# A chunked recurrence and an expert layer: products over a head's 40 entries, issued by groups of heads or alternating between two halves of the array's rows

## The chip, the core and the metric

The kernel runs on one core of a Trainium2 chip. The metric is the device time of one execution in microseconds, the median over runs of the same kernel. Engines are named as the profile names them: PE is TensorE (PEld its weight loads), DVE VectorE, ACT ScalarE, POOL GpSimd, SP SyncE, which here only issues DMAs.

## What is computed

Everything is float32. A recurrence (4 batches, 8 heads, 768 steps, 40 entries a head) carries a 40 x 40 state a head; its outputs, laid side by side, are 3072 tokens of 320 entries, and a two-level gate sends each token to one of 16 experts.

```python
for t in range(S):
    y[:, :, t] = np.einsum('bhd,bhde->bhe', rt, state)
    Sa = np.einsum('bhde,bhe->bhd', state, at)
    state_decay = state * wt[:, :, None, :] - np.einsum('bhd,bhe->bhde', Sa, bt)
    state = state_decay + np.einsum('bhd,bhe->bhde', vt, kt)
...
h = np.maximum(xg[mask_e] @ w1[g, e], 0.0)
ye = h @ w2[g, e]
out[tok_idx] = combined[:, None] * ye
```

## The kernel before

**Part one** computes the recurrence in chunks of 128 steps: 6 chunks a batch, 24 in all, the four batches taking turns. A chunk holds all 8 heads. The inputs of a chunk lie with a head's 40 entries on the partitions: even heads on partitions 0 to 39, odd heads on 64 to 103, four heads of each kind side by side along the free axis. `blk(g)` (L174) gives the partitions of the even (g = 0) or the odd heads (g = 1). A matmul over the 40 entries therefore uses the lower half of the array's rows for an even head and the upper half for an odd one.

`product` (L222) makes, for one of the two groups, four 128 x 128 matrices, one a head, in one PSUM bank (a tile of the tag `big`, of which five are in turn), and VectorE then multiplies the bank by a triangular mask into SBUF (L228). It is called eight times a chunk: for GT (L233), E (L235) and MT (L251) at the chunk's front, and for NT (L324) at its end. A float32 matmul stands in the trace as two passes, so the four matmuls of one call are eight records of PE and eight of PEld.

The other steps of a chunk, in the order in which PE takes them:

- The gate's logits of the chunk before: transposes of its tokens (L120) and small matmuls (L131). The scheduler sets the first products of the new chunk between them.
- The products GT and E; then the right-hand side (L260, L263), which needs GT with its mask.
- E's rows are summed, bounded and scaled (L239 to L244, VectorE and GpSimd), then E is transposed on PE (L247) and copied by ScalarE (L249).
- The product MT; then transposes of b, k and the running products (L217).
- Seven levels of the inverse: in each PE squares E and its transpose (L273, L282), ScalarE or VectorE copies the squares to SBUF, and PE applies the transposed square to U (L293), which VectorE adds up (L299).
- U is transposed (L304, copied at L307); the next state's products (L314, L315) go to VectorE, which updates the state ST (L318, L341) with qo (L320); the product NT needs the transposed U; the new state is transposed (L346).
- The chunk's outputs are summed from three products (L328, L332 with MT, L334 with NT) and scaled by VectorE (L336).

The tile framework's scheduler sets the order on each engine from the program's order and the dependences; the input loads of later chunks run on SP's queue, with three sets of input tiles in turn.

**Part two** chooses the experts (mostly VectorE), scatters the tokens by expert to DRAM, and then takes 39 tiles of 128 rows through the two expert matrices (L558, L566). The loops at L389 and L429 run zero times for these inputs.

Of the kernel before, what the change touches and what calls it, by code (L numbers as in the profile page):

```python
# [9 lines left out]
F32 = mybir.dt.float32  # L10
I32 = mybir.dt.int32
AX = mybir.AxisListType
ALU = mybir.AluOpType
# [3 lines left out]

# The chunked form of the recurrence divides by running products of w and inverts I + T by
# powers of T. Both are accurate while w stays within these bounds (128 factors make 1e-15 to
# 1e15) and no row of |T| sums to more than T_MAX. If an input breaks them anywhere, the  # L20
# recurrence is computed again a step at a time, in the reference's order.
W_MIN, W_MAX, T_MAX = 0.765, 1.3, 1.0
# [3 lines left out]
def kernel(  # L26
# [15 lines left out]
    nc = tc.nc  # L42
    P = 128
    B, H, D, S = rT.shape
    DM = H * D
    C = P
    NC = S // C
    NN = B * NC
    NP = H // 2
    HW = 64  # L50
    G, Eg = w1.shape[0], w1.shape[1]
# [7 lines left out]
    NK = len(KO)  # L59
    XW = DM + 2  # L60
    NT = (NTOK + NE * (P - 1)) // P
# [10 lines left out]
    def big(shape):  # L72
        return psum.tile(shape, F32, tag="big", name="big", bufs=5)
# [3 lines left out]

# [1 line left out]
    ident = cpool.tile([P, P], F32, name="ident")  # L79
    make_identity(nc, ident)  # L80
    ones = cpool.tile([P, P], F32, name="ones")
    nc.gpsimd.memset(ones, 1.0)
    # up[s, t] = 1 for s < t; low[t, s] = 1 for s < t
    up = cpool.tile([P, P], F32, name="up")
    nc.gpsimd.affine_select(out=up, in_=ones, compare_op=ALU.is_ge, fill=0.0, base=-1,
                            pattern=[[1, P]], channel_multiplier=-1)
    low = cpool.tile([P, P], F32, name="low")
    nc.gpsimd.affine_select(out=low, in_=ones, compare_op=ALU.is_ge, fill=0.0, base=-1,
                            pattern=[[-1, P]], channel_multiplier=1)
    up4 = up[:, None, :].broadcast_to([P, NP, P])  # L90
    low4 = low[:, None, :].broadcast_to([P, NP, P])

# [1 line left out]
    # A row of x_all is a token: its vector, its gate weight and its number.  # L94
    x_all = cpool.tile([P, NN, XW], F32, name="x_all")
# [8 lines left out]

    # Rows sorted by expert, each expert's share filled up to whole tiles. Rows that no token
    # takes keep a zero vector and a number beyond the last token.
    xs = dpool.tile([NT * P, XW], F32, name="xs")
# [8 lines left out]
    def transpose_x(pool, src):  # L116
        """[128 tokens, DM] -> [128, NK, 128 tokens]."""
        pt = big([P, NK, P])
        for ko, (k0, kn) in enumerate(KO):
            nc.tensor.transpose(pt[:kn, ko, :], src[:, k0:k0 + kn], ident)  # L120
        t = pool.tile([P, NK, P], F32, tag="xT", name="xT", bufs=2)
        nc.vector.tensor_copy(out=t[:, :NK - 1, :], in_=pt[:, :NK - 1, :])  # L122
        kn = KO[-1][1]
        nc.scalar.copy(out=t[:kn, NK - 1, :], in_=pt[:kn, NK - 1, :])  # L124
        return t
# [8 lines left out]

# [1 line left out]
    # With P_t the product of w over the chunk's steps before t and Q_t that product through t,  # L136
    # A = a P, K = k / Q, B = b / Q and S the state at the chunk's start:
    #   (I + T) U = A S' + G V,         T[t, s] = B_s . A_t,  G[t, s] = K_s . A_t   (s < t)
    #   Y = P (R S + M K - N B),        M[t, s] = r_t . v_s,  N[t, s] = r_t . u_s   (s < t)
    #   next S = (S + V' K - U' B) Q_last  # L140
    # and (I + T)^-1 = (I - T)(I + T^2)(I + T^4)... exactly, T being strictly triangular.
    with ExitStack() as part:
# [14 lines left out]
        for i in range(2):  # L157
            t = pers.tile([P, H, HW], F32, name=f"U{i}")
            nc.gpsimd.memset(t[:, :, D:], 0.0)
            U_pad.append(t)  # L160
        # The states of a pair of heads stand as the two diagonal blocks of a square that is zero
        # elsewhere: ST with the second axis of a state on the partitions, SN with the first.
        ST, SN = [], []
# [10 lines left out]
        def blk(h):  # L174
            return slice((h % 2) * HW, (h % 2) * HW + D)

        for u in range(NN):
# [4 lines left out]
            if u < NB:  # L182
                # the partitions that no head's rows take
                for nm in "wakbvr":
                    for q0 in (32, 96):
                        nc.any.memset(d[nm][q0:q0 + 32], 1.0 if nm == "w" else 0.0)
                nc.any.memset(d["pq"][:, :, 0:1], 1.0)
# [9 lines left out]

            # the running products of w (within its bounds), and a, k, b scaled by them
            nc.vector.tensor_reduce(out=w_max[:, n:n + 1], in_=d["w"], axis=AX.XY, op=ALU.max)
# [21 lines left out]

            def product(lhs, rhs, g, mask, name, bufs):  # L222
                ps = big([P, NP, P])
                for q in range(NP):
                    nc.tensor.matmul(ps[:, q, :], lhsT=lhs[blk(g), q, :], rhs=rhs[blk(g), q, :],  # L225
                                     start=True, stop=True)
                t = sb.tile([P, NP, P], F32, name=name, bufs=bufs)
                nc.vector.tensor_tensor(t, ps, mask, op=ALU.mult)  # L228
                return t

            # group 0 has the even heads, group 1 the odd ones
            GR = range(2)
            GT = [product(Kt, At, g, up4, "GT", 4) for g in GR]  # L233
            # T and its transpose; a row beyond its bound is scaled down to it
            E = [product(At, Bt, g, low4, "E", 6) for g in GR]  # L235
            ET = []
            for g in GR:
# [12 lines left out]
                ET.append(t)  # L250
            MT = [product(Vt, Rt, g, up4, "MT", 4) for g in GR]  # L251
            nB = natural(Bt, "nB", -1.0)
            Kn = natural(Kt, "Kn", 1.0)
            Pn = natural(Pm, "Pn", 1.0)

            # the right-hand side, then a factor of the inverse at a time
            ps = small([P, H, D])
# [50 lines left out]

            # the next state
            if c < NC - 1:  # L310
# [11 lines left out]

            # what the chunk returns
            NTm = [product(UT, Rt, g, up4, "NT", 4) for g in GR]  # L324
            ps = small([P, H, D])
# [25 lines left out]

        # how often the bounds are broken
        bad = pers.tile([P, 4], F32, name="bad")
# [13 lines left out]

# [1 line left out]
    with ExitStack() as part:  # L369
# [4 lines left out]
        BH = B * H  # L374
        # partition (q, b, h) holds rows q DQ .. (q + 1) DQ of the state of (b, h)
        st = sq.tile([P, DQ, D], F32, name="st")
# [56 lines left out]

# [1 line left out]
    with ExitStack() as part:  # L435
# [12 lines left out]
        def choose(vals, name):  # L448
            """The first largest of each token's values as a one-hot, and its softmax weight."""
            sh = [P, NN, G]  # L450
# [32 lines left out]

        # each token's rank within its expert, then its row in xs
        ohf = oh.rearrange("p n e -> p (n e)")
# [31 lines left out]

        # each tile's expert
        past = gp.tile([P, NT, NE], F32, name="past")
# [11 lines left out]

# [1 line left out]
    with ExitStack() as part:  # L533
# [66 lines left out]
```

## Time and profile before

| | |
|---|---|
| median of the runs shown (2 runs: 2348.99 and 2349.27 us) | 2349.13 us |
| the profiled execution: span from the first to the last instruction | 2344.1 us |
| of that, PE's matmuls busy | 2137.4 us (91%) |
| VectorE, ScalarE, GpSimd busy | 636.2, 416.2, 188.8 us |
| mean granted clock of PE | 0.806 |

The span is the profiled execution's own time; what lies around it is the difference to the median, 5 us. A record of PE begins when its pass begins; its end is modelled, and consecutive passes overlap in the records, so the pace of a stage is read from the starts. The granted clock is a share of the full 2.4 GHz: 0.50 is 1.2 GHz.

### The profile page before, as it was taken

Reading aid. Unit: us, or ns where it says so; the run is one execution under the profiler, and the core shown is the slowest. Engines: PE = TensorE matmul, PEld = TensorE weight load, DVE = VectorE, ACT = ScalarE, POOL = GpSimd, SP = SyncE. Lnnn points to the kernel's source line nnn. Section 1 sums busy time; section 2 is a strip of 40 time slices with the busy share of each in tenths; the row PEclk is TensorE's granted clock in tenths of the full one; section 3 lists DMA queues with packets and bytes.
Section 4 is the critical chain, followed back from the end, with each engine's and each line's share of the span. In section 5 each row is a group of like instructions: output and inputs, shape, how many; then the busy total and the mean of one; then the engine's idle time right before and its main releaser. Section 6 shows DMA issues by size and latency. Waiting matters only on the chain. (4 is left out here: it accounts for less than half of the span.)

```text
span 2344.1 us, 32451 instructions
## 1 busy us (share of the span) xinstructions
PE 2137.4 (91%) x13731; PEld 1943.0 (83%) x13731; DVE 636.2 (27%) x1156; ACT 416.2 (18%) x766; POOL 188.8 (8%) x190
## 2 busy tenths in 40 slices
PE   4999999999999999999999999999505999999998
PEld 3999999999999999999999999999404677777676
DVE  6423333332333333233333232222300111111111
ACT  2222222121222212122212122222000000000000
POOL 3000000000000000000000000000021000000000
PEclk9878876687877868787767787777656999999999
DMA  6000000000000000000000000000042666666661
GB/s 186 21 12 18 21 17 19 20 18 12 18 18 18 21 21 18 12 18 18 18 21 18 12 13 18 4 1 1 29 155 88 212 212 215 200 202 217 205 212 51
DMA packets 143699, 152.68 MB, mean 65 GB/s; under 512 B 33529, under 2 KB 129534, under 8 KB 143552
## 3 DMA queue, kind: packets, MB, share of 16 engines
q1 hardware_dynamic: 133824, 136.21, 18.9%
q10 hardware_dynamic: 6704, 6.46, 1.0%
q0 software_dynamic: 3024, 7.90, 0.9%
q8 instruction: 111, 1.82, 0.3%
q14 instruction: 36, 0.29, 0.0%
HBM read 136.22 MB, written 16.78 MB: 65 GB/s over the span
## 5 line engine op out<-in xcount | busy, mean ns | idle before, releaser
L558 PE MATMUL big<-xT,w1s 128*128 128x128 f32 x1872 | 338.9, 312 | 25.3 <-DVE xT L122 24.6
L558 PEld LDWEIGHTS big<-xT,w1s 128*128 128x128 f32 x1872 | 259.3, 191 | 108.0 <-DVE xT L122 34.7
L293 PE MATMUL small<-U,ET 128*128 128x40 f32 x2688 | 345.9, 290 | 0.6 <-ACT ET L276 0.4
L293 PEld LDWEIGHTS small<-U,ET 128*128 128x128 f32 x2688 | 340.8, 205 | 2.3 <-ACT ET L276 0.5
L273 PE MATMUL big<-ET,E 128*128 128x128 f32 x2304 | 336.6, 292 | 0.0
L273 PEld LDWEIGHTS big<-ET,E 128*128 128x128 f32 x2304 | 300.7, 204 | 0.0
L282 PE MATMUL big<-E,ET 128*128 128x128 f32 x1920 | 266.0, 284 | 0.0
L276 ACT COPY ET<-big 128x512 f32<-128x512 f32 x288 | 168.8, 586 | 481.2 <-PE big L273 481.2
L282 PEld LDWEIGHTS big<-E,ET 128*128 128x128 f32 x1920 | 247.3, 201 | 0.0
L299 DVE TENSOR_TENSOR U<-U,small 128x320 f32<-128x320 f32 x168 | 80.7, 480 | 457.4 <-PE small L293 457.4
L566 PE MATMUL small<-w2s,hT 128*128 128x320 f32 x624 | 180.5, 443 | 0.0
L566 PEld LDWEIGHTS small<-w2s,hT 128*128 128x128 f32 x624 | 116.6, 192 | 48.9 <-issue 1.6
L244 POOL TENSOR_TENSOR E<-E,fit 128x512 f32<-128x512 f32 x48 | 48.9, 1039 | 1199.5 <-DVE fit L242 1188.8
L561 DVE TENSOR_SCALAR hT<-big 128x512 f32<-128x512 f32 x39 | 27.0, 692 | 342.6 <-PE big L558 342.6
L124 ACT COPY xT<-big 64x128 f32<-64x128 f32 x63 | 16.3, 259 | 565.2 <-DVE xT L122 565.2
L120 PE MATMUL big<-ident,xt 128*128 128x128 f32 (+1 forms) x117 | 19.6, 277 | 96.4 <-DMA xt<-xs 96.4
L225 PE MATMUL big<-in_a,in_k 40*128 40x128 f32 x384 | 89.0, 447 | 18.1 <-DMA in_r<-in_rT_dram 18.1
L120 PEld LDWEIGHTS big<-ident,xt 128*128 128x128 f32 (+1 forms) x117 | 14.2, 133 | 105.4 <-DMA xt<-xs 97.5
L334 PE MATMUL small<-nB,NT 128*128 128x40 f32 x384 | 98.6, 351 | 0.0
L225 PEld LDWEIGHTS big<-in_a,in_k 40*128 40x128 f32 x384 | 75.1, 322 | 27.8 <-POOL in_k L212 18.1
L332 PE MATMUL small<-Kn,MT 128*128 128x40 f32 x384 | 94.4, 339 | 0.0
L263 PE MATMUL small<-vn,GT 128*128 128x40 f32 x384 | 94.1, 402 | 0.0
(166 smaller groups left out, 2302.5 us busy)
## 6 DMA issues: line engine op xcount, KB each, us to landing
w2s<-in_w_dram SPq DMA_DIRECT2D x39, 1280.0 KB
w1s<-in_w_dram SPq DMA_DIRECT2D x39, 1024.0 KB
w1s<-in_w_dram SPq DMA_DIRECT2D x39, 256.0 KB
xs<-blank ACTq DMA_DIRECT2D x1, 6279.0 KB
xt<-xs SPq DMA_DIRECT2D x39, 161.0 KB
vn<-in_v_dram SPq DMA_DIRECT2D x24, 160.0 KB
in_w<-in_wT_dram SPq DMA_DIRECT2D x48, 80.0 KB
in_a<-in_aT_dram SPq DMA_DIRECT2D x48, 80.0 KB
```

Of the source, the lines that this page charges most:

```text
L225: nc.tensor.matmul(ps[:, q, :], lhsT=lhs[blk(g), q, :], rhs=rhs[blk(g), q, :], start=True, stop=True)
L244: nc.gpsimd.tensor_tensor(E[g], E[g], fit.broadcast_to([P, NP, P]), op=ALU.mult)
L263: nc.tensor.matmul(ps[:, 2 * i + j, :], lhsT=GT[j][:, i, :], rhs=vn[:, 2 * i + j, :], start=(c == 0), stop=(c == 0 or j == 1))
L273: nc.tensor.matmul(ps[:, q, :], lhsT=E[g][:, q, :], rhs=ET[g][:, q, :], start=True, stop=True)
L276: nc.scalar.copy(out=t, in_=ps)
L282: nc.tensor.matmul(ps[:, q, :], lhsT=ET[g][:, q, :], rhs=E[g][:, q, :], start=True, stop=True)
L293: nc.tensor.matmul(ps[:, h, :], lhsT=ET[h % 2][:, h // 2, :], rhs=U[:, h, :], start=True, stop=True)
L299: nc.vector.tensor_tensor(nx, U, ps, op=ALU.add if lv else ALU.subtract)
L332: nc.tensor.matmul(o, lhsT=MT[j][:, i, :], rhs=Kn[:, i, blk(j)], start=(c == 0), stop=False)
L334: nc.tensor.matmul(o, lhsT=NTm[j][:, i, :], rhs=nB[:, i, blk(j)], start=False, stop=(c == 0 or j == 1))
L558: nc.tensor.matmul(ps[:, f, :], lhsT=w1s[:kn, ko, (f0 + f) * P:(f0 + f + 1) * P], rhs=xT[:kn, ko, :], start=(ko == 0), stop=(ko == NK - 1))
L566: nc.tensor.matmul(ps, lhsT=hT[:, f, :], rhs=w2s[:, f, :], start=(f == 0), stop=(f == FQ - 1))
```

## The change

`product` no longer takes the group. It takes two PSUM banks at once, one for the even and one for the odd heads, and issues the eight matmuls head by head: even, odd, even, odd. When all eight stand in the program, the two masks follow. It returns both results, so the four places that called it twice call it once. The number of matmuls, masks and banks is the same. (The change also blanks comment lines, so line numbers behind `product` rise by 6: L263 becomes L269, L334 becomes L340; the matmuls of `product` stand at L228, the masks at L233.)

```diff
-            def product(lhs, rhs, g, mask, name, bufs):
-                ps = big([P, NP, P])
+            def product(lhs, rhs, mask, name, bufs):
+                pss = [big([P, NP, P]) for _ in range(2)]
                 for q in range(NP):
-                    nc.tensor.matmul(ps[:, q, :], lhsT=lhs[blk(g), q, :], rhs=rhs[blk(g), q, :],
-                                     start=True, stop=True)
-                t = sb.tile([P, NP, P], F32, name=name, bufs=bufs)
-                nc.vector.tensor_tensor(t, ps, mask, op=ALU.mult)
-                return t
+                    for g in range(2):
+                        nc.tensor.matmul(pss[g][:, q, :], lhsT=lhs[blk(g), q, :],
+                                         rhs=rhs[blk(g), q, :], start=True, stop=True)
+                out = []
+                for g in range(2):
+                    t = sb.tile([P, NP, P], F32, name=name, bufs=bufs)
+                    nc.vector.tensor_tensor(t, pss[g], mask, op=ALU.mult)
+                    out.append(t)
+                return out
...
-            GT = [product(Kt, At, g, up4, "GT", 4) for g in GR]
+            GT = product(Kt, At, up4, "GT", 4)
...
-            E = [product(At, Bt, g, low4, "E", 6) for g in GR]
+            E = product(At, Bt, low4, "E", 6)
...
-            MT = [product(Vt, Rt, g, up4, "MT", 4) for g in GR]
+            MT = product(Vt, Rt, up4, "MT", 4)
...
-            NTm = [product(UT, Rt, g, up4, "NT", 4) for g in GR]
+            NTm = product(UT, Rt, up4, "NT", 4)
```

The order of PE at GT and E of one chunk in the middle of the program (the products of in_a with in_k are GT, of in_b with in_a E; the numbers behind `big_` tell the banks' tiles apart), before:

```order
L225 MATMUL big_4061<-in_a0_98,in_k0_99 128x128 x3
L131 MATMUL small_4031<-wg_77,xT_4028 128x20 x2
L225 MATMUL big_4061<-in_a0_98,in_k0_99 128x128
L131 MATMUL small_4031<-wg_77,xT_4028 128x20
L225 MATMUL big_4068<-in_a0_98,in_k0_99 128x128 x4
L225 MATMUL big_4075<-in_b0_100,in_a0_98 128x128 x4
L225 MATMUL big_4082<-in_b0_100,in_a0_98 128x128 x4
```

and with the change, the first twelve rows of the same place:

```order
L228 MATMUL big_4061<-in_a0_98,in_k0_99 128x128
L228 MATMUL big_4062<-in_a0_98,in_k0_99 128x128
L228 MATMUL big_4061<-in_a0_98,in_k0_99 128x128
L131 MATMUL small_4031<-wg_77,xT_4028 128x20 x2
L228 MATMUL big_4062<-in_a0_98,in_k0_99 128x128
L131 MATMUL small_4031<-wg_77,xT_4028 128x20
L228 MATMUL big_4061<-in_a0_98,in_k0_99 128x128
L228 MATMUL big_4062<-in_a0_98,in_k0_99 128x128
L228 MATMUL big_4061<-in_a0_98,in_k0_99 128x128
L228 MATMUL big_4062<-in_a0_98,in_k0_99 128x128
L228 MATMUL big_4075<-in_b0_100,in_a0_98 128x128
L228 MATMUL big_4076<-in_b0_100,in_a0_98 128x128
```

The logits stay behind the third matmul, which is now one of the lower half again, and the halves alternate throughout; E follows in the same way.

The order of VectorE at the same place, from the masks of GT to the scale of E's rows, before:

```order
L228 TENSOR_TENSOR GT_4066<-big_4061,up_70 128x512
L228 TENSOR_TENSOR GT_4073<-big_4068,up_70 128x512
L228 TENSOR_TENSOR E_4080<-big_4075,low_72 128x512
L239 TENSOR_REDUCE t_sum_88<-E_4080 128x4
L228 TENSOR_TENSOR E_4087<-big_4082,low_72 128x512
L242 TENSOR_SCALAR fit_4090<-t_sum_88 128x4
L239 TENSOR_REDUCE t_sum_88<-E_4087 128x4
L243 RECIPROCAL fit_4090<-fit_4090 128x4
L242 TENSOR_SCALAR fit_4102<-t_sum_88 128x4
L243 RECIPROCAL fit_4102<-fit_4102 128x4
```

and with the change:

```order
L233 TENSOR_TENSOR GT_4071<-big_4061,up_70 128x512
L233 TENSOR_TENSOR GT_4073<-big_4062,up_70 128x512
L233 TENSOR_TENSOR E_4085<-big_4075,low_72 128x512
L233 TENSOR_TENSOR E_4087<-big_4076,low_72 128x512
L245 TENSOR_REDUCE t_sum_88<-E_4085 128x4
L245 TENSOR_REDUCE t_sum_88<-E_4087 128x4
L248 TENSOR_SCALAR fit_4090<-t_sum_88 128x4
L248 TENSOR_SCALAR fit_4102<-t_sum_88 128x4
L249 RECIPROCAL fit_4090<-fit_4090 128x4
L249 RECIPROCAL fit_4102<-fit_4102 128x4
```

The second mask of E moved ahead of the first reduction.

The order of PE behind NT at a chunk's end, before (`big_4018` holds the transposed state):

```order
L225 MATMUL big_3981<-in_r2_116,UT_3966 128x128 x4
L225 MATMUL big_3988<-in_r2_116,UT_3966 128x128 x4
L346 MATMUL big_4018<-ident_63,ST0_124 128x128
L334 MATMUL small_3995<-nB_3700,NT_3986 128x40
L332 MATMUL small_3995<-Kn_3707,MT_3693 128x40
L346 MATMUL big_4018<-ident_63,ST0_124 128x128 x3
L334 MATMUL small_3995<-nB_3700,NT_3993 128x40
```

and with the change, from the last two matmuls of NT:

```order
L228 MATMUL big_3981<-in_r2_116,UT_3966 128x128
L228 MATMUL big_3982<-in_r2_116,UT_3966 128x128
L352 MATMUL big_4018<-ident_63,ST0_124 128x128 x4
L340 MATMUL small_3995<-nB_3700,NT_3991 128x40
L338 MATMUL small_3995<-Kn_3707,MT_3693 128x40
L340 MATMUL small_3995<-nB_3700,NT_3993 128x40
```

All four transposes of the state now stand ahead of the first matmul that needs NT. On VectorE, qo (L320) stood between NT's two masks and now stands ahead of both.

## Rows read from the trace of the kernel before

**Rows 1.** The page: span, then busy time of the engines.

```profile
span 2344.1 us, 32451 instructions
PE 2137.4 (91%) x13731; PEld 1943.0 (83%) x13731; DVE 636.2 (27%) x1156; ACT 416.2 (18%) x766; POOL 188.8 (8%) x190
```

**Rows 2.** Windows, two chunks: us, busy us (PE, PEld, DVE, ACT, POOL), granted clock, DMA.

```profile
637.75:658.23 20.48, 20.01 (x101) 18.58 (x102) 7.00 (x15) 3.16 (x7) 2.04 (x2) 0.50 0.10 28
658.23:692.36 34.13, 33.55 (x300) 33.41 (x299) 13.73 (x20) 11.22 (x20) 2.94 (x2) 1.00 0.05 14
692.36:736.74 44.38, 43.80 (x216) 41.85 (x215) 15.88 (x26) 6.43 (x13) 4.98 (x4) 0.50 0.10 25
736.74:774.28 37.54, 36.80 (x327) 36.18 (x325) 9.77 (x19) 10.29 (x18) 0.00 (x0) 1.00 0.03 7
```

**Rows 3.** Windows by stage: GT with E, right-hand side, MT, NT; NT a chunk later.

```profile
639.05:645.65 6.60, 6.60 (x39) 6.11 (x38) 2.62 (x5) 0.44 (x2) 0.00 (x0) 0.50 0.00 0
645.65:650.79 5.14, 5.14 (x25) 5.14 (x25) 2.27 (x7) 0.00 (x0) 2.04 (x2) 0.50 0.00 0
...
652.67:655.69 3.02, 3.02 (x17) 2.79 (x16) 0.69 (x1) 0.59 (x1) 0.00 (x0) 0.50 0.03 6
...
695.41:698.44 3.03, 3.03 (x18) 2.80 (x17) 1.75 (x4) 0.00 (x0) 0.00 (x0) 0.50 0.31 54
...
767.69:769.33 1.64, 1.64 (x17) 1.52 (x16) 1.42 (x3) 0.00 (x0) 0.00 (x0) 1.00 0.33 59
```

**Rows 4.** Timeline of PE in GT and E (start, us, engine, line, operation).

```profile
639.05 1.65 PE L225 MATMUL big<-in_a,in_k 40*128 40x128 f32 x6
...
641.60 0.81 PE L225 MATMUL big<-in_a,in_k 40*128 40x128 f32 x4
...
642.63 0.58 PE L225 MATMUL big<-in_b,in_a 40*128 40x128 f32 x1
642.84 0.42 PE L225 MATMUL big<-in_a,in_k 40*128 40x128 f32 x1
643.00 0.42 PE L225 MATMUL big<-in_b,in_a 40*128 40x128 f32 x1
643.05 0.42 PE L225 MATMUL big<-in_a,in_k 40*128 40x128 f32 x1
643.22 0.42 PE L225 MATMUL big<-in_b,in_a 40*128 40x128 f32 x1
...
643.43 2.29 PE L225 MATMUL big<-in_b,in_a 40*128 40x128 f32 x13
```

**Rows 5.** Timeline of DVE at MT's masks.

```profile
654.78 0.69 DVE L228 TENSOR_TENSOR MT<-big,up 128x512 f32<-128x512 f32 x1 [6.82 <-PE big L225]
655.80 0.69 DVE L228 TENSOR_TENSOR MT<-big,up 128x512 f32<-128x512 f32 x1 [0.33 <-PE big L225]
```

**Rows 6.** Timeline at NT of the next chunk, where the clock is high.

```profile
768.33 0.49 DVE L341 TENSOR_TENSOR ST<-s,qo 128x320 f32<-128x320 f32 x1
768.89 0.69 DVE L228 TENSOR_TENSOR NT<-big,up 128x512 f32<-128x512 f32 x1
...
769.50 0.16 DVE L320 TENSOR_TENSOR qo<-pq,own 128x8 f32<-128x8 f32 x1
...
769.63 0.30 PEld L334 LDWEIGHTS small<-nB,NT 128*128 128x128 f32 x2 [0.16 <-DVE NT L228]
```

**Rows 7.** Timeline of E's reduction, small steps and scaling.

```profile
645.53 0.69 DVE L239 TENSOR_REDUCE t_sum<-E 128x4 f32<-128x512 f32 x1
...
647.78 0.18 DVE L243 RECIPROCAL fit<-fit 128x4 f32<-128x4 f32 x1
647.79 2.04 POOL L244 TENSOR_TENSOR E<-E,fit 128x512 f32<-128x512 f32 x2 [49.16 <-DVE fit L242]
```

**Rows 8.** Timeline of PE: the transposes behind MT, one chunk later than rows 3.

```profile
725.04 1.11 PE L217 MATMUL big<-ident,in_b 128*128 128x128 f32 x4
```

**Rows 9.** Window of an earlier stretch at the high clock, from its rise to its fall.

```profile
388.58:419.30 30.72, 30.14 (x270) 30.00 (x270) 7.38 (x14) 9.96 (x17) 1.19 (x1) 1.00 0.02 7
```

## The prediction

> **What bounds the kernel now.** I read the page's busy table first: TensorE's matmuls fill 91% of the span and its weight loads 83%, VectorE 27% [rows 1]. So only what TensorE issues, or waits for, can move the end. In the table of windows the reader is to see the second fact: TensorE's granted clock goes to and fro between 0.50 (1.2 GHz) and 1.00 (2.4 GHz), nearly once a chunk. Four windows in a row, 20.48 us low, 34.13 high, 44.38 low, 37.54 high, are two chunks: 136.53 us, 68.27 a chunk, of which 35.84 high and 32.43 low [rows 2]. TensorE is over 97% busy in all four, so in the recurrence nearly every microsecond is a TensorE instruction. Its work, counted at the full clock, is 35.84 + 32.43 / 2 = 52.05 us a chunk. The products stand in the low stretches: the windows by stage show 0.50 for GT with E (6.60 us) and for MT (3.02 us); for NT it is 3.03 us at 0.50 in one chunk and 1.64 us at 1.00 in the next [rows 3].
>
> Then the timeline of TensorE inside GT and E, because there it shows how the two halves behave [rows 4]. A matmul of float32 stands there as two passes, each a weight load and a matmul. Passes of one half follow at 0.21 us: 642.63, 643.00 (the first gap is longer), 643.22, 643.43 for E's even heads. But E's even heads (lower half) start at 642.63 while GT's odd heads (upper half) still start passes at 642.84 and 643.05. So the halves already run side by side where the program's order brings them close; each keeps its own pace of 0.21. What the grouped order loses is the lag before the second half may start. For MT VectorE shows it: the two masks, each waiting for its half, start at 654.78 and 655.80, 1.02 us apart [rows 5].
>
> The Trainium skill ("TensorE: Matmul & The Clock Gate", Part 3, "The mechanism") says that matmuls start and end strictly in program order. The trace differs: a pass of E at 642.63 comes before passes of GT that the program has ahead of it [rows 4]. By the rule the old order would have no overlap, 16 x 0.21 us, and alternating would win half of that, 1.7 us a product, 4 x 24 x 1.7 = 163 us; by the rows a good part of that is won already, the sum below goes by them, and the measurement decides.
>
> **The change, part by part.** Nothing is added or removed on any engine: the same 8 matmuls a product, the same two masks of 0.69 us. Moved are the matmuls within each product, VectorE's masks of E (now both ahead of the two reductions), NT's masks (behind qo), and the transposes of the state (all four ahead of NT's first use).
>
> MT, at the low clock. One half alone takes 7 x 0.213 = 1.49 us from its first pass to its last; the lag adds 1.02; from the last pass to the first transpose behind it (655.69) the remaining 0.51 us go by, the change to the whole array among it; sum 3.02 [rows 3, 5]. Alternating, the lag falls to between none and two pass gaps, 0.43 us: both halves can start at once, but the old lag of 1.02 is nearly five gaps, so only some five or six passes seem to be taken up ahead of time, and a hiccup of one gap is likely. I take 0.22, and save 0.80 us (bounds 0.59 and 1.02).
>
> GT with E. The scheduler puts parts of the gate's logits between GT's matmuls, so this is in two pieces [rows 4]. Six passes of one half, first at 639.05, stand ahead of the logits; now four lower and two upper ones do, two gaps fewer, 0.43 us. Behind the logits run 26 product passes and two half-array passes of the logits, with two lags left: from 641.60 to the last product pass (0.35 us before 645.65) 3.70 us, its first slow gap included. Now each half has 14 such passes, 13 x 0.213 = 2.78, plus the slow first gap and one hiccup, 3.2: 0.50 saved. Together 0.93 us (bounds 0.6 and 1.3).
>
> NT, at the low clock, is as MT, 0.80 us. Its masks come later in relation to the passes, as both halves end together; the four transposes of the state, 4 x 0.21 = 0.85 us, now stand ahead of the first use of NT and hide the first mask's 0.69; the second mask ends 0.69 later behind two more matmuls. In the last four chunks there are no such transposes, and I count a third. At the full clock the gain is nothing: VectorE does the state's two steps until 768.82 and only then NT's first mask (768.89), which L334 awaits at 769.63 [rows 6]; that was never held by TensorE, and qo, 0.16 us, now stands ahead of it, so this stage loses about 0.1. Counted along the timeline, fourteen of the 24 chunks have NT at the low clock, four of them with little gain; as a mean over 24, 0.80 x 10 / 24 + small change = 0.45 us.
>
> What is late next. In E's chain two masks and two reductions of 0.69 us, four small steps of up to 0.18 and GpSimd's two scalings, 2.04 together, lead to the transposes of E (650.79 in this chunk) [rows 3, 5, 7]. From the end of the passes that is 4 x 0.69 + 4 x 0.18 + 2.04 = 5.5 us for the second E, and a scaling less, 4.5, for the first. TensorE's cover is the right-hand side, 5.14 us [rows 3], plus 0.35 us of change and 0.85 of the first transposes. It holds by 0.8 us; were E's chain a microsecond longer, a chunk would lose 0.2, and as much for every 0.2 beyond. The transposes behind MT need E's banks, not MT's, so MT's mask stays off the path. A second PSUM bank is held for 8 matmuls longer; all five were already in turn, and their former readers end microseconds before.
>
> Sum at face value: 0.93 + 0.80 + 0.45 = 2.2 us a chunk, 24 chunks, 53 us. The experts' part has no product and stays.
>
> **What the clock makes of it.** The work saved is 2.2 us at half speed, 1.1 at the full clock, so 50.95 is left. With h us of high clock a chunk lasts h + 2 x (50.95 - h) = 101.9 - h. With the old mean h of 35.84: 66.1, the face value. With the longer of the two stretches, 37.54: 64.4, -94 us over 24 chunks. With the shorter, 34.13: 67.8, -12 us [rows 2]. The trace shows what sets h. In one chunk the clock rises at 658.23, 2.5 us after the transposes behind MT began (655.69); in the next at 736.74, 11.7 us after the same instruction (725.04) [rows 2, 3, 8]. So half of the chunks run a good part of their dense squarings at 1.2 GHz. The change makes the stage just ahead of them shorter and fuller, which speaks for an earlier rise, and nothing in it makes the squarings thinner. I take h = 36.8, between the old mean and the longer stretch: 65.1 us a chunk, 3.1 less, 24 x 3.1 = 74 us. This is the least certain term.
>
> The profiled execution spans 2344.1 us, 5 us below the median of 2349.13, which is what lies around the span; the saving is taken from the median: 2349 - 74 = 2275 us. A measurement of this kernel tells about 2% from no change, 47 us, so "faster" is below 2302.
>
> **Rivals.**
> Clock pattern unchanged or worse than the mean: the face value alone gives 2349 - 53 = 2296; with h = 34.13 2349 - 12 = 2337. For it: the pattern of rise and fall is none of the program's doing, and falls came as early as the end of the squarings (692.36). Against: the slow chunk has 9 us of rise to win.
>
> The alternation doesn't take: the halves wait for each other when they change with every matmul, so that passes come as before, 3.02 us a product, and the time stays at 2349. For it: no row shows more than a short run of alternating passes, some 3 of each half. Against: in that run each half keeps its 0.21.
>
> Slower: the clock locks into its poorest pattern. One stretch of the trace is high for 30.72 us only [rows 9]. If every chunk had h = 30.7, it would last 101.9 - 30.7 = 71.2 us, 2.9 more than now: 2349 + 70 = 2419 us. It decides from h below 33.6. For it: chunks with such a stretch exist among the 24. Against: they are few, and a shorter front doesn't lead there.
>
> A full win: no hiccup, lags gone, h = 37.5. Front 1.3 + 1.02 + 0.6 = 2.9 us a chunk, 1.45 of work; 101.2 - 37.5 = 63.7, 4.6 less, 110 us: 2239.
>
> **How the numbers follow.** Forecast with h above the old mean (2255 to 2296) 0.55; full win 0.15; clock as before or worse than the mean (2296 to 2337) 0.20, half of it close to 2296; no alternation 0.06; slower by the clock 0.04. Faster than 2302: the first two and half of the third, 0.80; within 2%: 0.16; slower: 0.04. The range from 2235 to 2318 takes the full win, the forecast and the better part of the third.
>
> **What would show it.** Right: in MT both masks wait for TensorE until nearly the same time (the second starts right behind the first, 0.69 later), and MT's stage takes about 2.2 us at 0.50; GT with E about 5.7; NT about 2.2 at 0.50 and no shorter at 1.00; TensorE still over 95% busy; chunks near 65 us. Wrong: MT's stage above 2.6 us (the halves don't alternate freely), a wait of L247 for GpSimd in most chunks (E's chain lost its cover), or stages that shrink as worked out while chunks stay at 67 to 68 us (the clock took it back).

## The result, and the profile after

The changed kernel takes **2267.29 us** (two runs, 2265.77 and 2268.81) beside 2349.13 before: a ratio of **0.9656, 95% interval 0.9638 to 0.9674**, 82 us or 3.4% faster. The prediction was 2275, range 2235 to 2318. (Ratios here and below leave out runs more than 1.5% above the fastest of their kernel; where that matters, the runs are listed.)

The page of the changed kernel, span and busy time, answering to [rows 1]:

```profile
span 2266.8 us, 32427 instructions
PE 2053.1 (91%) x13731; PEld 1853.9 (82%) x13731; DVE 624.8 (28%) x1156; ACT 415.6 (18%) x766; POOL 188.8 (8%) x190
```

The same 13731 matmuls, and TensorE's share is still 91%: its busy time fell by 84 us, the span by 77. Now the stages, in the order GT with E, right-hand side, MT (windows: stretch, us, busy us of PE, PEld, DVE, ACT, POOL, granted clock, DMA share and GB/s), answering to [rows 3]:

```profile
678.08:683.49 5.41, 5.41 (x40) 4.92 (x39) 1.71 (x3) 0.43 (x2) 0.00 (x0) 0.50 0.01 3
683.49:688.63 5.14, 5.14 (x27) 5.14 (x25) 2.89 (x8) 0.00 (x0) 2.03 (x2) 0.50 0.00 0
690.50:692.51 2.01, 2.01 (x17) 1.79 (x16) 0.00 (x0) 0.59 (x1) 0.00 (x0) 0.50 0.00 0
```

GT with E went from 6.60 to 5.41 us and MT from 3.02 to 2.01; the right-hand side between them is 5.14 as before. NT, from the timelines of TensorE at the low clock, first before, then after:

```profile
695.41 3.09 PE L225 MATMUL big<-in_r,UT 40*128 40x128 f32 x16
698.44 0.47 PE L346 MATMUL big<-ident,ST 128*128 128x128 f32 x1
698.70 0.49 PE L334 MATMUL small<-nB,NT 128*128 128x40 f32 x2
```

```profile
471.96 2.08 PE L228 MATMUL big<-in_r,UT 40*128 40x128 f32 x16
473.97 1.11 PE L352 MATMUL big<-ident,ST 128*128 128x128 f32 x4
474.88 0.59 PE L340 MATMUL small<-nB,NT 128*128 128x40 f32 x2
```

The time from NT's first pass to the first transpose of the state went from 3.03 to 2.01 us, and that to the first use of NT from 3.29 to 2.92, with all four transposes ahead of it instead of one. At the high clock the passes are shorter too (1.64 us to the first transpose, now 1.27), but NT's first use comes no sooner: 1.94 us after the first pass before (767.69 to 769.63), 1.98 now (735.13 to 737.11). Why MT is shorter, VectorE's timeline at its masks says, the counterpart of [rows 5]:

```profile
692.62 1.29 DVE L233 TENSOR_TENSOR MT<-big,up 128x512 f32<-128x512 f32 x2 [6.06 <-PE big L228]
```

The two masks are one unbroken group now: one wait for TensorE, then both, back to back. Before, the second began 1.02 us after the first and waited for TensorE again. That lag of the upper half is what the change removed.

The clock, two chunks in a row, cut where it changes, answering to [rows 2]:

```profile
676.79:704.10 27.31, 26.86 (x144) 25.43 (x144) 12.96 (x21) 5.12 (x11) 4.98 (x4) 0.50 0.12 34
704.10:741.64 37.54, 36.60 (x327) 35.78 (x326) 9.78 (x19) 10.40 (x18) 0.00 (x0) 1.00 0.04 8
741.64:768.95 27.31, 26.90 (x144) 25.47 (x145) 12.93 (x21) 5.17 (x11) 4.99 (x4) 0.50 0.11 34
768.95:806.50 37.55, 36.58 (x327) 35.75 (x326) 9.82 (x19) 10.35 (x18) 0.00 (x0) 1.00 0.04 8
```

Both chunks read alike, 27.31 + 37.54 = 64.85 us, and so do twelve chunks in a row; the others have 30.72 to 40.96 us high. Before, two unlike chunks took turns here (20.48 low and 34.13 high, then 44.38 low and 37.54 high; 68.27 a chunk).

**Splitting the gain.** The view of the cores gives the span and the mean granted clock; first before, then after:

```profile
core 0: 2344.1 us, clock 0.806
```

```profile
core 0: 2266.8 us, clock 0.822
```

With W = span x mean clock, the work in microseconds of full clock (waits included), and H the time at the high clock, a span is 2W - H. Before: W = 2344.1 x 0.806 = 1889, H = 3779 - 2344 = 1435. After: W = 1863, H = 1460. The clock is rounded to 0.001, so W is good to about 1 us and H to 2. Of the 77 us that the span lost, twice 26 = 52 is work, and 25 is more time at the high clock. Over all runs on record (40 of the kernel before, 8 of the changed one) W is 1885 to 1891 and 1862 to 1867, and on the mean W fell by 23 and H rose by 37. So some 47 to 52 of the 82 us are work, and 25 to 37 are clock. All experiments are read by this split.

### The profile page after: what moved, and what is told of

It is laid out like the page before. It is cut to its first block, busy times and chain, and to the rows that moved or that the text cites. A ratio compares the mean times of both kernels' runs of the same rounds, so it can differ in the third digit from the quotient of the medians.

```text
span 2266.8 us, 32427 instructions
## 1 busy us (share of the span) xinstructions
PE 2053.1 (91%) x13731; PEld 1853.9 (82%) x13731; DVE 624.8 (28%) x1156; ACT 415.6 (18%) x766; POOL 188.8 (8%) x190
## 5 line engine op out<-in xcount | busy, mean ns | idle before, releaser
L279 PE MATMUL big<-ET,E 128*128 128x128 f32 x2304 | 344.5, 297 | 0.0
L279 PEld LDWEIGHTS big<-ET,E 128*128 128x128 f32 x2304 | 308.3, 208 | 0.0
L288 PE MATMUL big<-E,ET 128*128 128x128 f32 x1920 | 271.3, 288 | 0.0
L288 PEld LDWEIGHTS big<-E,ET 128*128 128x128 f32 x1920 | 252.9, 205 | 0.0
L340 PE MATMUL small<-nB,NT 128*128 128x40 f32 x384 | 93.0, 333 | 4.3 <-DVE NT L233 3.1
L292 ACT COPY E<-big 128x512 f32<-128x512 f32 x144 | 84.3, 585 | 55.5 <-PE big L288 55.5
L269 PE MATMUL small<-vn,GT 128*128 128x40 f32 x384 | 94.1, 402 | 0.0
L294 DVE COPY E<-big 128x512 f32<-128x512 f32 x96 | 66.4, 691 | 97.9 <-PE big L288 96.5
L269 PEld LDWEIGHTS small<-vn,GT 128*128 128x128 f32 x384 | 91.8, 333 | 0.9 <-issue 0.9
```

Of the source, the lines that this page charges most:

```text
L269: nc.tensor.matmul(ps[:, 2 * i + j, :], lhsT=GT[j][:, i, :], rhs=vn[:, 2 * i + j, :], start=(c == 0), stop=(c == 0 or j == 1))
L279: nc.tensor.matmul(ps[:, q, :], lhsT=E[g][:, q, :], rhs=ET[g][:, q, :], start=True, stop=True)
L288: nc.tensor.matmul(ps[:, q, :], lhsT=ET[g][:, q, :], rhs=E[g][:, q, :], start=True, stop=True)
L292: nc.scalar.copy(out=t, in_=ps)
L294: nc.vector.tensor_copy(out=t, in_=ps)
L340: nc.tensor.matmul(o, lhsT=NTm[j][:, i, :], rhs=nB[:, i, blk(j)], start=False, stop=(c == 0 or j == 1))
```

## The experiments

Each is a variant of the changed kernel unless it says "before with". W and H are of its profiled run; the time is the median of all its timed runs, and the ratio, taken as above, is against runs of the kernel before on the same chip (medians 2344.79 to 2351.69).

| kernel | time, us | ratio (95%) | W | H |
|---|---|---|---|---|
| before | 2349.13 | 1 | 1889 | 1435 |
| changed | 2267.29 | 0.9656 (0.9638 to 0.9674) | 1863 | 1460 |
| e1, all in the lower half | 2452.60 | 1.0451 (1.0410 to 1.0492) | 1931 | 1421 |
| e2, grouped, masks behind | 2350.10 | 0.9991 (0.9969 to 1.0013) | 1887 | 1418 |
| e3, before with GT and E alone | 2324.11 | 0.9880 (0.9841 to 0.9919) | 1875 | 1418 |
| e4, before with MT alone | 2265.36 | 0.9633 (0.9568 to 0.9698) | 1885 | 1515 |
| e5, the change again | 2267.87 | 0.9650 (0.9622 to 0.9677) | 1866 | 1467 |
| e6, alternating by two | 2305.41 | 0.9735 (0.9672 to 0.9799) | 1855 | 1397 |
| e7, E's chain 2.5 us longer | 2325.94 | 0.9917 (0.9886 to 0.9949) | 1873 | 1425 |
| e8, 12 more transposes a chunk | 2292.56 | 0.9777 (0.9747 to 0.9807) | 1890 | 1500 |
| e9, before with NT alone | 2391.92 | 1.0163 (1.0123 to 1.0203) | 1871 | 1350 |
| e10, MT right behind E | 2222.89 | 0.9460 (0.9433 to 0.9486) | 1851 | 1482 |
| e11, NT grouped again | 2282.50 | 0.9739 (0.9718 to 0.9759) | 1867 | 1452 |
| e12, e10 with NT grouped | 2278.45 | 0.9738 (0.9696 to 0.9780) | 1849 | 1429 |

**e1 and e2: is it the two halves, or the order of masks and banks?** e1 lets the odd heads' matmuls read the even heads' rows, so every pass lies in the lower half; the odd heads' results are left out of what is computed.

```diff
-                        nc.tensor.matmul(pss[g][:, q, :], lhsT=lhs[blk(g), q, :],
-                                         rhs=rhs[blk(g), q, :], start=True, stop=True)
+                        nc.tensor.matmul(pss[g][:, q, :], lhsT=lhs[blk(0), q, :],
+                                         rhs=rhs[blk(0), q, :], start=True, stop=True)
```

> The alternating kernel, but the matmuls of the odd heads read the even heads' rows too, so all eight of a product use the lower half of the array's rows (the products of the odd heads are replaced by those of the even ones; banks, masks and order stay as in the changed kernel). Theory (the gain is that the two halves run side by side): with one half all 16 passes follow each other at 0.213 us at the low clock, so MT's stage takes 15 x 0.213 + 0.55 = 3.7 us (2.01 in the changed kernel, 3.02 before), GT with E about 8.8 (5.4 and 6.6), and the kernel is slower than before: 3.6 us a chunk, 2349 + 87 = 2436 us, give or take 40 for the clock's pattern. Rival (the gain comes of the masks' and transposes' new places): near 2267.

e2 keeps the new `product` with both banks and late masks, and only swaps the loops back.

```diff
-                for q in range(NP):
-                    for g in range(2):
+                for g in range(2):
+                    for q in range(NP):
```

> Both banks at once and both masks behind all eight matmuls, as in the changed kernel, but the matmuls again group by group. Theory (alternation alone pays): the stages are those of before, MT 3.0 us with a lag of 1.0 between the halves, and the time is 2349 us, give or take 25 for the clock's pattern. Rival (masks' places and bank use pay): near 2267.

e1, timeline at MT:

```profile
756.22 3.78 PE L228 MATMUL big<-in_r,in_v 40*128 40x128 f32 x16
...
759.93 0.90 PE L217 MATMUL big<-ident,in_b 128*128 128x128 f32 x3
```

e2, VectorE at the same place:

```profile
723.97 0.69 DVE L233 TENSOR_TENSOR MT<-big,up 128x512 f32<-128x512 f32 x1 [6.83 <-PE big L228]
724.99 0.69 DVE L233 TENSOR_TENSOR MT<-big,up 128x512 f32<-128x512 f32 x1 [0.33 <-PE big L228]
```

With one half alone MT takes 759.93 - 756.22 = 3.71 us; grouped by halves 3.02 (721.86 to 724.88 in e2), with the lag of 1.02 back; alternating 2.01. In e1 GT with E takes 8.82 us, and both times are as expected. So the halves do run side by side, the grouped order had a good part of that already, and banks and masks in their new places are worth nothing (0.9991). Shown.

**e3, e4 and e9: one product at a time.** The kernel before, with the new function used at one place and the old one elsewhere: GT and E (e3), MT (e4), NT (e9).

```diff
-            MT = [product(Vt, Rt, g, up4, "MT", 4) for g in GR]
+            MT = product2(Vt, Rt, up4, "MT", 4)
```

> Only GT and E alternate, MT and NT as before. Its stage is 5.4 us (6.6 before), MT stays at 3.0. Additive theory (each product brings its share of the 82 us by its own stage, 1.19 of 2.6 us a chunk): 2349 - 37 = 2312 us. Clock theory (a chunk's length is 2 x work - high time, and the high time settles by the pattern, not by the share): work falls by 0.6 us a chunk, the time anywhere from 2260 to 2340, over 10 us from 2312 more likely than not.

> Only MT alternates, GT, E and NT as before. Its stage is 2.0 us (3.02 before), GT with E stays at 6.6. Additive theory: 1.0 of 2.6 us a chunk, 2349 - 32 = 2317 us. Clock theory: work falls by 0.5 us a chunk, the face value is 2325, the time from 2290 to 2345 by the high time that it settles at.

> Only NT alternates. Where the clock is low at NT its stage to the outputs' end is 0.8 us shorter, where it is high nothing changes, since VectorE's state steps hold NT's masks there. Additive theory: 14 of 24 chunks by 0.8 us, 11 us, 2338. Rival (NT's new place of qo and of the state's transposes costs at the high clock what it gains at the low): 2349, within 5.

The stages shrink as in the whole change (MT in e4 takes 2.01 us, 688.98 to 690.99, beside GT with E at the old 6.61); e3, window of GT with E:

```profile
630.70:636.11 5.41, 5.41 (x39) 4.92 (x39) 1.71 (x3) 0.43 (x2) 0.00 (x0) 0.50 0.00 0
```

The times don't add up: -26, -85 and +40, each against the kernel before on its own chip, make -71, where all three together give -82, and NT alone is *slower* than before. e3 came out 12 us from its additive theory; e4 and e9 lie outside what either of their theories gave. In work each is a saving: W is 14, 4 and 18 us below 1889. The clock makes the rest. e4, two chunks cut where the clock changes:

```profile
613.22:630.29 17.07, 16.49 (x92) 15.13 (x90) 5.38 (x12) 2.03 (x5) 2.04 (x2) 0.50 0.07 20
630.29:674.66 44.37, 43.21 (x385) 42.46 (x384) 18.01 (x28) 13.29 (x23) 2.94 (x2) 1.00 0.08 22
674.66:701.97 27.31, 27.31 (x141) 25.88 (x142) 12.84 (x20) 4.99 (x10) 4.98 (x4) 0.50 0.10 28
701.97:739.51 37.54, 36.96 (x330) 36.45 (x329) 9.64 (x18) 10.53 (x18) 0.00 (x0) 1.00 0.04 10
```

e9, the same:

```profile
706.62:747.58 40.96, 40.38 (x204) 38.30 (x203) 15.87 (x26) 5.58 (x11) 3.98 (x4) 0.50 0.09 25
747.58:778.30 30.72, 30.14 (x269) 30.00 (x269) 7.31 (x13) 9.95 (x17) 1.00 (x1) 1.00 0.02 6
```

e4 has up to 44.37 us of a chunk at the high clock, e9 30.72: over the span H = 1515 against 1350. e4's four runs were 2253.26, 2256.41, 2274.32 and 2334.38, at mean clocks of 0.837, 0.836, 0.828 and 0.803: the same program, 81 us apart, and the clock moves with it. Their W are 1884, 1885, 1881 and 1873, so W itself grows a little with H, 12 us for 102 us of H, as it would if waits lasted as long at either clock (not tested). So a microsecond more at the high clock is worth about 1 - 2 x 0.12 = 0.76. With that slope, and each at the H of before, the savings of work are 12 (GT and E), 14 (MT) and 8 (NT), and 29 for the whole change. NT's part was measured with NT at the low clock in 21 of the 24 chunks (e9); in the changed kernel it is there in 7, a third, so 3 of its 8 are left, and 12 + 14 + 3 make the 29. The parts add up in work, within the 2 or 3 us by which W varies from run to run, and not at all in time.

**e5: the change again**, unedited, for the spread.

> The changed kernel itself, more runs, to see how far one kernel's times spread and with what high time. If the clock's pattern is set by the program alone, all runs lie within 0.3% (2260 to 2274). If it also depends on when a run begins, as the runs with MT alone suggest (2253 to 2334 us at mean clocks of 0.837 to 0.803), they spread by 1% or more, and the median may be some 20 us off 2267.

Six runs from 2256.64 to 2270.55, a spread of 0.6%, between what the two answers gave, so the question stays open. W lies between 1862 and 1867, H between 1456 and 1479; the median, 2267.87, is within 1 us of the first two runs.

**e6: how far ahead does a half look?** Two matmuls of one half, then two of the other.

```diff
-                for q in range(NP):
-                    for g in range(2):
-                        nc.tensor.matmul(pss[g][:, q, :], lhsT=lhs[blk(g), q, :],
-                                         rhs=rhs[blk(g), q, :], start=True, stop=True)
+                for q, g in ((0, 0), (1, 0), (0, 1), (1, 1), (2, 0), (3, 0), (2, 1), (3, 1)):
+                    nc.tensor.matmul(pss[g][:, q, :], lhsT=lhs[blk(g), q, :],
+                                     rhs=rhs[blk(g), q, :], start=True, stop=True)
```

> The halves alternate by two matmuls: two even, two odd, two even, two odd. Theory (about six passes are taken up ahead of time): the second half starts at once, as only four passes stand ahead of it, but each half falls behind once, by one gap of 0.21; MT's stage 2.2 to 2.45 us (2.01 alternating, 3.02 grouped). Rival (a half is let in only when it changes with every matmul): 3.0 us. Rival (any order with the second half within the first eight passes will do): 2.01. The whole time is left to the clock's pattern, 2255 to 2330.

e6, windows of MT and of GT with E:

```profile
705.35:707.52 2.17, 2.17 (x18) 1.95 (x17) 0.06 (x1) 0.58 (x1) 0.00 (x0) 0.50 0.00 0
...
692.75:698.32 5.57, 5.57 (x39) 5.08 (x38) 1.71 (x3) 0.43 (x2) 0.00 (x0) 0.50 0.01 3
```

2.17 and 5.57 us, 0.16 above strict alternation, where eight passes of one half in a row cost 1.0: just below the expected 2.2, and neither rival. The second half's first pass begins 0.01 us behind the first half's, so it does start at once. The 0.16 is one long gap, 0.37 us in place of 0.21, between the fifth and the sixth pass of one half.

How far a half looks ahead, the trace of the kernel before tells: when E's first pass began at 642.63, three passes of GT were still to begin, at 642.84 and 643.05 [rows 4] and here:

```profile
643.26 0.42 PE L225 MATMUL big<-in_a,in_k 40*128 40x128 f32 x1
```

At MT it is the same: five passes of the first half begin, which takes 0.37 + 3 x 0.21 = 1.0 us, the lag; then the second half's first begins, and then the first half's last three. So what is seen is a look-ahead of three passes, not of six. In e6, too, three passes of the first half are still to begin when the second half starts.

e6's time fits no stage sum (its profiled run is the longest of the four): runs of 2269.04, 2301.80, 2309.02 and 2315.18 at H = 1464, 1421, 1398 and 1397.

**e7: the cover of E's chain.** One more GpSimd multiplication, by ones, behind each scaling of E.

```diff
                 nc.gpsimd.tensor_tensor(E[g], E[g], fit.broadcast_to([P, NP, P]), op=ALU.mult)
+                nc.gpsimd.tensor_tensor(E[g], E[g], ones[:, None, :].broadcast_to([P, NP, P]),
+                                        op=ALU.mult)
```

> The changed kernel with one more GpSimd multiplication by ones behind each scaling of E, so that E's second transposes must wait: 1.3 us more of idle TensorE a chunk and not one instruction more on it. Additive theory: 24 x 1.3 = 31 us, 2298. Clock theory: the chunk's length follows the pattern that the high time settles at; with the 36.9 us of high time a chunk kept, 2298 too, but with 34.4, as in the kernel where only GT and E alternate, 2360.

e7, the transposes of E on TensorE's timeline:

```profile
713.57 0.99 PE L271 MATMUL small<-vn,GT 128*128 128x40 f32 x4
715.65 2.34 PE L255 MATMUL big<-ident,E 128*128 128x128 f32 x8 [1.08 <-POOL E L251]
717.91 0.80 PE L228 MATMUL big<-in_r,in_v 40*128 40x128 f32 x4
```

TensorE now waits 1.08 us for GpSimd ahead of these transposes, and again inside them: from the last matmuls of the right-hand side to MT it takes 4.34 us, in the changed kernel 2.66 (687.84 to 690.50). The two added multiplications take 1.26 us each and lengthen the chain of the second E by 2.5; its transposes come 1.6 later, so its cover was about 0.9 us (predicted: 0.8). The time rose by 59 us, between the two theories. The longer stage accounts for 24 x 1.68 = 40 of them, and H fell from 1460 to 1425.

**e8: would denser work raise the clock sooner?** The transposes of b that open the squarings' stretch are done four times over.

```diff
-            nB = natural(Bt, "nB", -1.0)
+            nB = natural(Bt, "nB", -1.0, 4)
```

> The changed kernel with the transposes of b made four times instead of once, 12 dense passes more a chunk just ahead of the squarings, which nothing needs. Additive theory: 12 x 0.213 = 2.6 us a chunk at the low clock, 2267 + 61 = 2328 us. Clock theory: the stage ahead of the squarings is fuller, so the clock rises earlier; with 4 us more high time a chunk (as where MT alone alternates, 40.8) the 1.3 us of added work cost 2.6 and give back 4, 2267 - 34 = 2233 us.

e8, three stretches cut where the clock changes, and the first of the transposes in question:

```profile
627.50:668.46 40.96, 40.19 (x362) 39.49 (x361) 16.39 (x25) 12.71 (x22) 2.95 (x2) 1.00 0.07 17
668.46:692.35 23.89, 23.30 (x129) 21.73 (x128) 6.39 (x14) 3.22 (x7) 2.03 (x2) 0.50 0.07 21
692.35:726.48 34.13, 33.55 (x300) 33.40 (x299) 13.99 (x20) 11.64 (x20) 2.94 (x2) 1.00 0.06 16
```

```profile
687.99 3.68 PE L218 MATMUL big<-ident,in_b 128*128 128x128 f32 x16
```

The rise does come sooner, 4.4 us behind the start of these transposes (687.99 to 692.35) instead of 11.6 (in the changed kernel, from the transposes at 692.52 to 704.10). But the fall moves as well: of the 24 chunks ten are high for 34.13 us and eleven for 40.96 or 44.37, where the changed kernel has 37.54 in fourteen. Over its four runs W is 1885 to 1890 and H 1471 to 1500, on the mean 22 and 18 above the changed kernel's eight runs. So the earlier rise did bring high time, but under 1 us a chunk instead of the 4 of the clock theory, and the added work cost more: 25 us net, between the two theories.

**e10, e11 and e12: where MT stands, and what NT's alternation is worth.** e10 moves one line, so that GT, E and MT are one run of 48 half-array passes and E's transposes stand right ahead of those of b:

```diff
             E = product(At, Bt, low4, "E", 6)
+            MT = product(Vt, Rt, up4, "MT", 4)
...
-            MT = product(Vt, Rt, up4, "MT", 4)
             nB = natural(Bt, "nB", -1.0)
```

> The changed kernel with MT right behind E, so that GT, E and MT are one run of half-array passes. Two changes between half and whole array go (0.35 us each in place of 0.21) and one slow first gap (0.16): 0.4 us a chunk at the low clock, 10 us at face value, 2257. Rival (MT's masks now stand ahead of E's chain on VectorE, or MT waits for a bank): E's chain is later by 1.3 us, its cover longer by 0, TensorE waits for it, 2280 or more. The clock's pattern may add 40 either way.

e11 is the changed kernel with NT in the old function, e12 is e10 with the same:

```diff
-            NTm = product(UT, Rt, up4, "NT", 4)
+            NTm = [grouped(UT, Rt, g, up4, "NT", 4) for g in GR]
```

> The changed kernel with NT grouped again (GT, E and MT alternate). Additive theory from the parts alone (NT alone cost 42 us): 2267 - 42 = 2225 us. Stage theory (NT's stage gains 0.8 us at the low clock and nothing at the high, where the changed kernel mostly has it): 2267, within 10. Clock theory: NT's effect has no fixed sign; the time follows the high time that the chunks settle at, 2225 to 2320.

> MT right behind E, GT, E and MT alternating, NT grouped. If NT's alternation helps only by the low clock's stage, this is some 5 us slower than with it, 2228; if NT costs 42 us as it did alone, 2181.

e10, the moved line on TensorE's timeline, then two chunks cut by the clock:

```profile
664.11 1.92 PE L228 MATMUL big<-in_b,in_a 40*128 40x128 f32 x16
...
665.81 1.92 PE L228 MATMUL big<-in_r,in_v 40*128 40x128 f32 x16
...
667.66 0.71 PE L266 MATMUL small<-ST,in_a 128*128 128x80 f32 x2
...
672.80 1.95 PE L254 MATMUL big<-ident,E 128*128 128x128 f32 x8
...
674.54 0.63 PE L217 MATMUL big<-ident,in_b 128*128 128x128 f32 x2
```

```profile
589.89:610.37 20.48, 19.89 (x114) 18.87 (x114) 6.33 (x14) 3.18 (x7) 2.04 (x2) 0.50 0.08 24
610.37:644.50 34.13, 33.55 (x301) 33.41 (x300) 14.00 (x20) 11.69 (x21) 2.95 (x2) 1.00 0.06 16
644.50:675.22 30.72, 30.14 (x167) 28.61 (x168) 8.77 (x19) 3.00 (x7) 2.04 (x2) 0.50 0.09 22
675.22:716.18 40.96, 40.19 (x362) 39.49 (x360) 16.34 (x25) 12.91 (x23) 2.95 (x2) 1.00 0.07 17
```

**e10 is the fastest version: 2222.89 us, 0.9460 of before, 2% below the change** (expected: 2257, give or take 40 for the clock). No wait for GpSimd is shown at 672.80, so E's cover holds. MT's first pass comes 1.70 us after E's; the rise (675.22) comes 0.7 us behind the start of b's transposes. W is 12 below the changed kernel, H 22 above. The rows here account for some 5 of the 12 (0.31 us at MT and 0.14 at E's transposes, 24 chunks, counted half as the clock is low); the rest I did not trace.

Against e11, NT's alternation is worth 15 us, against e12 56 (0.8% and 2.8% by the ratios); alone in e9 it cost 40. e11 lies 15 us above its stage theory and inside the wide range of the clock theory; nothing forecast e12 (2181 or 2228, measured 2278). In e11 NT's edit changes W by 4 and H by 8; in e12 by 2 and 53. In e12 20 of the 24 chunks have 34.13 us high, in e10 14:

```profile
686.91:721.04 34.13, 33.64 (x301) 33.49 (x299) 13.95 (x20) 11.95 (x21) 2.94 (x2) 1.00 0.05 16
721.04:755.18 34.14, 33.46 (x179) 32.07 (x179) 9.75 (x23) 4.70 (x10) 2.04 (x2) 0.50 0.09 25
```

## Why the prediction was right, point by point

- **Lag, not overlap, is what is won: right.** e1 against e2 shows it: 3.71, 3.02 and 2.01 us for one half, grouped and alternating. The Trainium skill ("TensorE: Matmul & The Clock Gate", Part 3, "The mechanism") has matmuls start and end strictly in order; by that the grouped order would have cost nearly as much as e1 (an estimate), and the runs show it 0.7 us a product cheaper.
- **MT, 0.80 saved: mis-sized.** Measured 1.01, the upper bound given (1.02). The hiccup of one pass gap that I assumed doesn't occur. I had read the lag as a look-ahead of five or six passes; five is the number of passes that begin before the second half, and three, those still to begin, is the look-ahead seen (e6). Strict alternation never has more than the two passes of one matmul ahead of the other half. A hiccup shows in e6, with 0.16 us.
- **GT with E, 0.93: mis-sized in the same way.** Measured 1.19, inside 0.6 to 1.3.
- **NT, 0.80 at the low clock and nothing at the high: right for a chunk, wrong in the count.** e9 saves 8 us of W, 16 at the low clock, in 21 chunks with NT there: 0.8 us in each. At the high clock TensorE waits for the masks, as said, and NT's first use comes 0.04 us later (I said 0.1); timeline of TensorE and VectorE there, the counterpart of [rows 6]:

```profile
735.13 1.16 PE L228 MATMUL big<-in_r,UT 40*128 40x128 f32 x16
735.76 0.49 DVE L347 TENSOR_TENSOR ST<-s,qo 128x320 f32<-128x320 f32 x1
...
736.37 1.28 DVE L233 TENSOR_TENSOR NT<-big,up 128x512 f32<-128x512 f32 x2
736.40 0.63 PE L352 MATMUL big<-ident,ST 128*128 128x128 f32 x4
737.11 0.30 PEld L340 LDWEIGHTS small<-nB,NT 128*128 128x128 f32 x2 [0.32 <-DVE NT L233]
```

  But the count moved with the clock: NT begins at the low clock in 14 of the 24 chunks before, as I said, and in 7 now. So this term is about 0.8 x 7 / 24 = 0.23 us a chunk instead of 0.45.
- **The sum, 53 us at face value: near, by errors that partly cancel.** MT and GT with E give 24 x (1.01 + 1.19) = 53 alone, NT some 5 more, 58; W at the H of before gives 2 x 29 = 58 as well. MT and GT with E brought 0.47 us a chunk more than forecast, NT 0.22 less.
- **E's cover holds: right.** The second scaling ends at 688.64, and the second E's transposes begin at 689.52, so the margin is 0.9 us (0.8 predicted), and e7 says the same. Of the 24 chunks five have transposes of E that wait for GpSimd: the first two, as before, and three early ones for 0.57 us each. Timeline of GpSimd and TensorE, answering to [rows 7]:

```profile
686.60 2.04 POOL L250 TENSOR_TENSOR E<-E,fit 128x512 f32<-128x512 f32 x2 [48.78 <-DVE fit L249]
688.63 0.67 PE L253 MATMUL big<-ident,E 128*128 128x128 f32 x2
```

- **The clock, h = 36.8 by an earlier rise: the number held, the reason fell.** The predicted 21 us beyond the face value came as 25 in the profiled runs and as 37 over all runs. But the rise comes at 704.10, 11.6 us behind the transposes at 692.52, as late as in the slower of the two old chunks (11.7). What changed is the fall: it no longer comes at the end of the squarings in every second chunk (692.36 in [rows 2]) but late, as at 741.64, in 15 of the 24 chunks (before in 10). Over all chunks but the first it is the same: the rise comes on the mean 8.9 us behind the transposes of b (before: 7.5), the fall 3.3 us behind NT's first pass (before: 1.0). So I had the wrong end of the stretch, and that the number held is luck. e8 did make the rise earlier, to a mean of 3.5 us, and won under 1 us of high time a chunk.
- **The rivals.** "No alternation" fell by the stages. "Clock as before" and "full win" would each have been met by a neighbour of this kernel: e3 has H = 1418 and is slow for its work, e4 has 1515. The slower rival, a lock into the poorest pattern, did not come here, but it is real: e9 has 17 of 24 chunks with 30.72 us high and runs 1.6% slower than before with less work to do. I gave it 0.04 on the ground that a shorter front doesn't lead there; with NT alone the clock got there.
- **Open:** what makes the clock settle in one pattern rather than another. No theory of mine forecast H in e4, e6, e9, e11 or e12. Also open are why one run of e4 took 2334, and most of what e10 saves.

## What to carry to other kernels

Where matmuls use half of the array's rows, write those of the two halves alternately: even where the halves already overlap in the grouped order, each change of group left a lag of about a microsecond at 1.2 GHz, which the timeline shows and the busy table doesn't. In e10 it paid to put such products next to each other, though only part of its 44 us is traced. On a kernel whose clock rises and falls once a loop, split a result into work and high-clock time before believing it; a saving in a thin stage can be doubled or reversed by the clock, so measure combinations and don't add up parts.

## What the runs showed of the hardware that was not expected

- The time between a rise and a fall of TensorE's clock takes a few values in the chunks of all kernels here (30.72, 34.13, 37.54, 40.96 and 44.37 us a stretch), and it alone moved the time of kernels with nearly equal work by some 50 us: the profiled runs of e12 and e10 differ by 2 us in W and by 49 in span. TensorE is over 97% busy in low stretches too [rows 2].
- A kernel with less work can be slower: e9 saves 18 us of W and loses 85 of H.
- Passes of one half can begin ahead of passes of the other that stand before them in the program, three of them in the places looked at (642.63 in the kernel before, MT, e6). So two halves need not alternate strictly: by two matmuls they lose 0.16 us a product at the low clock, by four 1.0.
